# x by wide DMA transposes, the last w1/w3 columns with tokens on partitions, and a new order of the first loads

## The chip, the cores and the metric

The kernel runs on one core of a Trainium2 chip. Each core has five engines that work side by side: TensorE (PE; its weight loads are listed as PEld), VectorE (DVE), ScalarE (ACT), GpSimd (POOL) and SyncE (SP, which here only issues DMAs). Matrix products land in PSUM, from where ScalarE or VectorE must fetch them; DMAs move data between HBM and SBUF. The metric is the device time of one execution in microseconds; the time of a kernel is the median of its runs.

## The reference

Two branches share one input and a learned gate mixes them. All arrays are bf16; S = 2048 tokens, D = 512, F = 1376.

```
x = A_x                                              # [1, 2048, 512]
g = sigmoid((x * gate_w).sum(-1))                    # one number per token
q, k, v = x @ wqkv                                   # 32 heads of 16
a = softmax(mask(q k^T / 4)) v @ wo                  # mask: the last 256 keys, causal
b = (silu(x @ w1) * (x @ w3)) @ w2                   # F = 1376
out = g * a + (1 - g) * b
```

## The kernel before

**Layout.** Everything is computed from xT, x with its 512 features on partitions (four groups of 128, `NDC`) and the 2048 tokens along the free dimension. Tokens are handled in four parts of 512 (`t` or `g`).

- *Projections* (`add_proj`, `add_v`): Q and K come out transposed, 128 features (8 heads, a group `c`) by 512 tokens; V comes out with tokens on partitions. Each is four matmuls of 512 columns, one for each feature group of x. Only in the very first Q and K block, the 512 columns are done as twice 256, so that they can begin with half of the tokens (`spans`).
- *Scores* (`add_burst`): a "burst" is 8 to 12 small matmuls, four row groups of PE at a time, that fill a PSUM tile `big` of four banks. There is only one such tile. ScalarE takes the exponential of 2048 columns at once (L579), POOL or VectorE masks the edges of the window (L170, L589).
- *PV* (`add_pv`): the probabilities times V, 72 or 96 small matmuls; VectorE transposes the result and divides by the sum.
- *MLP* (`add_up`, `add_down`): F is cut into 11 pieces of 128 (`NFC`), the last of 96 (`FL`). For each piece and each 512 tokens, w1 and w3 are the stationary weights, and x's 512 tokens stream past: a tile of F on partitions by tokens, four matmuls each (L447). ScalarE forms tanh(gate/2) (L459), VectorE multiplies twice (L464, L469) and leaves a tile `hT`. The down product then uses 128 tokens of each `hT` as weights and streams w2 past (L502), 11 matmuls for each 128 tokens; piece 10 is last in order in the first part of the tokens, fifth in the others (`FSEQ`).
- *Gate*: `gate_w` is loaded as one more column of w1, so in the last piece 97 columns are used, and row 96 of the tanh tile `ttz` holds the gate's tanh for 512 tokens. It lies along the free dimension, and is needed with tokens on partitions. `add_gate` sends it to DRAM and back through two small DMAs on SP (L410, L414).
- *Output* (`add_out`): the product with wo, then one VectorE instruction that adds the two branches, and a store on SP (L541).

**How x gets transposed.** The first 512 tokens come as two tiles `xs` of 256 tokens in three plain DMAs (`x_dma`, L114); PE transposes them against an identity in 16 matmuls of 128 columns (`add_tx`, L238), and ScalarE and VectorE copy the results to xT (L244, L246). The three other parts come by DMA transpose straight into xT, four instructions of 512 tokens by 128 features each (`xt_dma`, L118).

**What sets the order.** The instruction order of all engines is written out by the kernel's own planner when the program is built. Each piece of work is an `Op` with engines, a planned duration, dependencies, and slots of pools that it takes and releases; `place` simulates the engines and takes the next op by a key. The planner's random moves (`MOVES`, `move`) shift the keys of single ops, and a list of seeds is fixed in the code. The loads have planned landing times (`dma(name, queue, time, ...)`, L133 to L152), which don't bind the chip: on the chip, an engine waits for the semaphore of the DMA. All these first loads are issued by SP in the order in which they stand: x, the first 128 columns of Q's and K's weights (q0, k0), V's weights (v), the rest of Q's and K's (kq), the first 512 columns of w1 and w3 (wa), their rest (wb), then x's part 1 (t1), w2, parts 2 and 3. An SP or ACT queue carries eight semaphores in turn, so that a DMA also waits for the one eight places before it.

While the first loads are under way, PE runs matmuls on constants (`idle_matmuls`, `NWARM` = 10 ahead, `NFILL` = 3 between the first transposes).

Of the kernel before, what the change touches and what calls it, by code (L numbers as in the profile page):

```python
# [19 lines left out]
def kernel(  # L20
# [38 lines left out]
    ident = pp.tile([P, P], BF16, name="ident")  # L59
    w2_sb = pp.tile([P, NFC, D], BF16, name="w2_sb")  # L60
    bsb = pp.tile([P, NT, D], BF16, name="bsb")
    w1_sb = pp.tile([P, NDC, F + 1], BF16, name="w1_sb")
    w3_sb = pp.tile([P, NDC, F], BF16, name="w3_sb")
# [4 lines left out]
    lim = pp.tile([P, 2, 1, HB], BF16, name="lim")  # L68
    scr = pp.tile([P, 2], F32, name="scr")
# [5 lines left out]
    dr = ctx.enter_context(tc.tile_pool(name="dr", bufs=1, space=bass.MemoryType.DRAM))  # L75
    zd = dr.tile([NTC, 512], F32, name="zd")
# [31 lines left out]
    xs_tiles = {}  # L108

    def x_dma(h, m0, m1):  # L110

        if h not in xs_tiles:
            xs_tiles[h] = xp.tile([P, 2, D], BF16, name=f"xs{h}")
        nc.sync.dma_start(out=xs_tiles[h][:, m0:m1, :],  # L114
                      in_=x2d[256 * h + P * m0:256 * h + P * m1, :].rearrange("(m p) d -> p m d", p=P))

    def xt_dma(t, c):
        nc.sync.dma_start_transpose(out=xT[:, c, 512 * t:512 * (t + 1)],  # L118
                                    in_=x2d[512 * t:512 * (t + 1), c * P:(c + 1) * P])

    def w_dma(eng, dst, src, lo, hi, base=0):
        eng.dma_start(out=dst[:, :, lo:hi],  # L122
                      in_=src[:, base + lo:base + hi].rearrange("(c p) f -> p c f", p=P))

# [3 lines left out]
    def dma(name, eng, at, fn):  # L128
# [4 lines left out]
    dma("x0a", "SP", 3.0, lambda: x_dma(0, 0, 1))  # L133
    dma("x0b", "SP", 3.55, lambda: x_dma(0, 1, 2))
    dma("q0", "SP", 4.2, lambda: w_dma(nc.sync, wq_sb, A_wqkv, 0, P))
    dma("x1", "SP", 4.9, lambda: x_dma(1, 0, 2))
    dma("k0", "SP", 5.5, lambda: w_dma(nc.sync, wk_sb, A_wqkv, 0, P, D))
    dma("v", "SP", 7.0, lambda: w_dma(nc.sync, wv_sb, A_wqkv, 0, D, 2 * D))
    dma("kq", "SP", 9.8, lambda: (w_dma(nc.sync, wk_sb, A_wqkv, P, D, D),
                                   w_dma(nc.sync, wq_sb, A_wqkv, P, D)))  # L140
# [3 lines left out]
    dma("wb", "SP", 17.5, lambda: (w_dma(nc.sync, w1_sb, B_w1, FA, F),  # L144
                                   w_dma(nc.sync, w3_sb, B_w3, FA, F)))
    dma("t1", "SP", 20.8, lambda: [xt_dma(1, c) for c in range(NDC)])
    dma("w2", "SP", 24.8, lambda: (
# [3 lines left out]
    dma("t2", "SP", 27.1, lambda: [xt_dma(2, c) for c in range(NDC)])  # L151
    dma("t3", "SP", 29.6, lambda: [xt_dma(3, c) for c in range(NDC)])  # L152
# [21 lines left out]
    def begin():  # L174

        nc.vector.memset(scr[:], 0.0)
        for fn in first_loads:
            fn()
        nc.scalar.activation(out=scr[:, 1:2], in_=scr[:, 0:1], func=ACT.Tanh)
        nc.gpsimd.memset(ident[:], 0.0)  # L180
        nc.gpsimd.affine_select(out=ident[:], in_=ident[:], pattern=[[-1, P]],
                                compare_op=ALU.not_equal, fill=1.0, base=0, channel_multiplier=1)
# [9 lines left out]
        nc.gpsimd.memset(Vaug[:, :, VW - DH:], 1.0)  # L192

# [32 lines left out]
    xT_op = {}  # L226

    def add_tx(m2):

        xT_op[m2] = []  # L230
        for j in range(2):
            key = ("tx", m2, j)
            hold("g", key, 1)

            def pe(key=key, j=j):
                tx = bank(key, BF16, (P, NDC, P))
                for c in range(NDC):
                    nc.tensor.transpose(out=tx[:, c, :], in_=xs_tiles[m2][:, j, c * P:(c + 1) * P],  # L238
                                        identity=ident[:])

            def evac(eng, key=key, j=j):
                dst = xT[:, :, (2 * m2 + j) * P:(2 * m2 + j + 1) * P]
                if eng == "ACT":
                    nc.scalar.copy(out=dst, in_=g_tile[key][:])  # L244
                else:
                    nc.vector.tensor_copy(out=dst, in_=g_tile[key][:])  # L246

            a = Op("PE", 0.22, pe, [loads["x1" if m2 else "x0b" if j else "x0a"]], acq=[("g", key)],
                   kind="tx")
            if (m2, j) == (0, 1):  # L250
                Op("PE", 0.107 * NFILL, lambda: idle_matmuls(NFILL), [a], kind="idle")
            xT_op[m2].append(Op("DVE" if j else "ACT", 0.43 if j else 0.59, evac, [a],
                                rel=[("g", key)], rank=-1))

    def xdep(t0, t1):

        r = []
        for c in range(NDC):
            r.append([xT_op[m // 2][m % 2] if m < 4 else loads[f"t{m // 4}"]
                      for m in range(t0 // P, t1 // P)])  # L260
        return r
# [55 lines left out]
    def add_proj(c, t, is_q):  # L317
# [5 lines left out]

        spans = [(0, 256), (256, 512)] if blk == (0, 0) else [(0, 512)]

        def pe(n0, n1, dc):
            def fn():
                b = bank(key) if (n0, dc) == (0, 0) else g_tile[key]
                nc.tensor.matmul(b[:, n0:n1], lhsT=(wq_sb if is_q else wk_sb)[:, dc, c * P:(c + 1) * P],  # L329
# [39 lines left out]
    def add_v(m):  # L369
# [32 lines left out]
        return a0  # L402

    gate_op = {}
    def add_gate(t, b, tl, row):

        st = {}

# [534 lines left out]
```

## Time and profile before

| What | us |
|---|---|
| Median of 3 runs | 235.07 (234.72 to 235.4) |
| The profiled execution | 234.09 |
| Its span, from the first instruction to the last | 232.4 |
| PE busy | 222.7 (96%) |
| ScalarE busy | 185.5 (80%) |
| VectorE busy | 174.8 (75%) |
| POOL busy | 166.0 (71%) |

The span is cut into 40 slices on the page; a digit is the busy share of an engine in tenths. Groups of instructions are listed as line, engine, operation, output and inputs, shape and count, then busy time in us, the mean of one in ns, and the idle time of the engine before them with what ended it. "issue" is idle time for which the profile shows no cause. A matmul's listed duration runs from its start to its end; matmuls overlap, so that the spacing of their starts is what one costs in a row of them. Rows of the timeline give the start, the time until the last one ends, and how many were merged. Rows "SPq" are DMA issues: the time that SP's sequencer spends on issuing, not the transfer.

### The profile page before, as it was taken

The numbers are of one execution on the slowest core, as the hardware profiler recorded it, in microseconds if no ns is written. First come the engines' busy times: TensorE is split into PE (matmuls) and PEld (weight loads), VectorE is DVE, ScalarE is ACT, GpSimd is POOL, SyncE is SP. The second block draws the span as 40 slices with busy tenths as digits, with TensorE's granted clock in tenths as the row PEclk, the third lists the DMA queues.
The fourth block names the chain that finished last, engine by engine and source line by source line (L and its number), as shares of the span: only waits on it lengthen the run. The fifth ranks groups of instructions, "written<-read, shape, count | busy, mean of one in ns | idle before, by whom it ended". The sixth has DMA issues, their size and how long they took to land.

```text
span 232.4 us, 6996 instructions
## 1 busy us (share of the span) xinstructions
PE 222.7 (96%) x2952; PEld 102.2 (44%) x2985; DVE 174.8 (75%) x296; ACT 185.5 (80%) x169; POOL 166.0 (71%) x323
## 2 busy tenths in 40 slices
PE   7999999999999999999999999999999999999993
PEld 4544443544344443544444444434444444444442
DVE  1497989897999697769969587688978765785622
ACT  3699798998988988987978899897988988893121
POOL 8076688888889887797769777777877879783000
PEclk9999999999999999999999999999999999999999
DMA  5999962000000000000000000000000001000001
GB/s 147 335 367 160 245 131 77 4 1 3 0 25 4 0 13 15 3 24 3 24 3 25 1 3 23 6 23 3 0 27 3 23 4 25 3 25 0 25 34 58
DMA packets 18424, 10.99 MB, mean 47 GB/s; under 512 B 10228, under 2 KB 18388, under 8 KB 18392
## 3 DMA queue, kind: packets, MB, share of 16 engines
q1 hardware_dynamic: 18360, 10.54, 18.4%
q8 instruction: 23, 0.38, 0.7%
q14 instruction: 9, 0.07, 0.1%
q0 software_dynamic: 32, 0.00, 0.1%
HBM read 6.86 MB, written 2.11 MB: 39 GB/s over the span
## 4 chain that ended last, share of the span: by engine, by line
PE 92%; issue 2%; DMA 2%; DVE 1%; SPq 1%; DVEq 0%
PE g L447 34%; PE g L502 16%; PE g L329 12%; PE big L569 11%; PE g L617 8%; PE g L377 6%; PE g L531 5%; DMA wv_sb<-in_A_wqkv_dram 2%; SPq L114 1%; DVE kz L343 1%; SPq L122 0%; DVE ot L538 0%; DVE Vaug L393 0%; DVEq L938 0%; DVEq L538 0%
## 5 line engine op out<-in xcount | busy, mean ns | idle before, releaser
L170 POOL TENSOR_SCALAR_AFFINE_SELECT e<-e 64x256 bf16<-64x256 bf16 (+1 forms) x306 | 160.3, 524 | 44.4 <-ACT e L579 28.2
L579 ACT ACTIVATE e<-big 128x2048 bf16<-128x2048 f32 x76 | 141.0, 1855 | 18.9 <-PE big L569 16.2
L447 PE MATMUL g<-xT,w_sb 128*128 128x512 bf16 (+2 forms) x340 | 84.8, 380 | 2.1 <-issue 1.7
L447 PEld LDWEIGHTS <-w_sb 128*128 128x128 bf16 (+2 forms) x352 | 32.6, 100 | 39.5 <-issue 7.4
L502 PE MATMUL g<-w_sb,hT 128*128 128x512 bf16 (+1 forms) x163 | 40.2, 379 | 1.5 <-issue 1.4
L469 DVE TENSOR_TENSOR hT<-h,g 128x512 bf16<-128x512 bf16 (+1 forms) x44 | 29.8, 680 | 4.4 <-PE g L447 1.6
L628 DVE STREAM_TRANSPOSE t<-g 128x512 f32<-128x512 f32 x32 | 21.4, 698 | 12.8 <-PE g L617 12.8
L464 DVE SCALAR_TENSOR_TENSOR h<-tt,g 128x512 bf16<-128x512 bf16 x40 | 27.0, 682 | 4.1 <-ACT tt L459 3.7
L569 PE MATMUL big<-qp,kz 32*128 32x320 bf16 (+2 forms) x720 | 30.0, 254 | 0.0
L459 ACT ACTIVATE tt<-g 128x512 bf16<-128x512 f32 x40 | 23.5, 596 | 1.8 <-PE g L447 1.5
L502 PEld LDWEIGHTS <-hT 128*128 128x128 bf16 (+1 forms) x176 | 16.1, 97 | 19.7 <-issue 1.1
L569 PEld LDWEIGHTS <-kz 32*128 32x128 bf16 x720 | 10.7, 92 | 31.8 <-issue 31.0
L343 DVE TENSOR_TENSOR kz<-g,maskEO 128x1024 bf16<-128x1024 f32 x16 | 19.5, 1219 | 2.4 <-PE g L329 2.1
L589 DVE TENSOR_TENSOR e<-e,lim 128x256 bf16<-128x256 bf16 x31 | 10.2, 329 | 13.5 <-ACT e L579 13.4
L617 PE MATMUL g<-e,Vaug 64*32 64x320 bf16 (+4 forms) x1440 | 20.3, 253 | 0.0
L508 ACT ACTIVATE bsb<-g,omg 128x512 bf16<-128x512 f32 x13 | 8.9, 686 | 14.1 <-PE g L502 14.0
L393 DVE CAST Vaug<-g 64x256 bf16<-64x256 f32 x40 | 17.1, 427 | 2.9 <-PE g L377 1.9
L617 PEld LDWEIGHTS <-Vaug 64*32 64x32 bf16 x1440 | 16.6, 91 | 3.8 <-issue 1.9
L329 PE MATMUL g<-xT,wq_sb 128*128 128x512 bf16 (+1 forms) x65 | 17.3, 367 | 0.4 <-issue 0.2
L329 PE MATMUL g<-xT,wk_sb 128*128 128x512 bf16 (+1 forms) x65 | 17.2, 367 | 0.3 <-issue 0.2
L538 DVE SCALAR_TENSOR_TENSOR ot<-g,gq,bsb 128x512 bf16<-128x512 f32 (+1 forms) x17 | 11.8, 703 | 7.3 <-PE g L531 5.0
L531 PE MATMUL g<-xs,OT 128*128 128x512 bf16 (+1 forms) x68 | 16.3, 366 | 0.0
(41 smaller groups left out, 117.7 us busy)
## 6 DMA issues: line engine op xcount, KB each, us to landing
out_dram<-ot SPq DMA_DIRECT2D x15, 128.0 KB, 1.7
w_sb<-in_B_w_dram SPq DMA_DIRECT2D x2, 864.0 KB, 10.1
w_sb<-in_B_w_dram SPq DMA_DIRECT2D x1, 1280.0 KB, 6.7
w_sb<-in_B_w_dram SPq DMA_DIRECT2D x2, 512.0 KB, 8.2
wv_sb<-in_A_wqkv_dram SPq DMA_DIRECT2D x1, 512.0 KB
xs<-in_A_wo_dram SPq DMA_DIRECT2D x2, 256.0 KB, 3.0
wk_sb<-in_A_wqkv_dram SPq DMA_DIRECT2D x1, 384.0 KB, 6.1
wq_sb<-in_A_wqkv_dram SPq DMA_DIRECT2D x1, 384.0 KB
```

Source lines behind the costliest of these rows:

```text
L170: nc.gpsimd.affine_select(out=part, in_=part, pattern=[[0, n], [sgn, HB]], compare_op=ALU.is_ge, fill=0.0, base=0 if kind == 0 else -1, ch ...
L329: nc.tensor.matmul(b[:, n0:n1], lhsT=(wq_sb if is_q else wk_sb)[:, dc, c * P:(c + 1) * P], rhs=xT[:, dc, 512 * t + n0:512 * t + n1], start ...
L343: nc.vector.tensor_tensor(out=dst[:], in0=src.to_broadcast(shape), in1=maskEO[:].to_broadcast(shape), op=ALU.mult)
L447: nc.tensor.matmul(b[0:m, :], lhsT=wsb[:, dc, f * P:f * P + m], rhs=xT[:, dc, t * 512:(t + 1) * 512], start=(dc == 0), stop=(dc == NDC - 1))
L459: nc.scalar.activation(out=tl["tt"][0:m, :], in_=g_tile[kg][0:m, :], func=ACT.Tanh, scale=0.5)
L464: nc.vector.scalar_tensor_tensor(out=tl["h1"][0:fs, :], in0=tl["tt"][0:fs, :], scalar=1.0, in1=g_tile[kg][0:fs, :], op0=ALU.add, op1=ALU.mult)
L469: nc.vector.tensor_tensor(out=h_tile[(t, f)][0:fs, :], in0=tl["h1"][0:fs, :], in1=g_tile[ku][0:fs, :], op=ALU.mult)
L502: nc.tensor.matmul(b[:], lhsT=h_tile[(t, f)][0:fs, (m % 4) * P:(m % 4 + 1) * P], rhs=w2_sb[0:fs, f, :], start=(n == 0), stop=(n == NFC - 1))
L531: nc.tensor.matmul(b[:, 0:n], lhsT=OT_tile[m // 4][:, c, (m % 4) * P:(m % 4 + 1) * P], rhs=wo_t[c // 2][:, c % 2, n0:n1], start=(c == 0), ...
L569: nc.tensor.matmul(big[:, u, s0:s0 + step * (w - 1) + 1:step, :], lhsT=k_tile[(c, j // 8)][32 * u:32 * u + 32, j % 8].rearrange("p i x -> ...
L579: nc.scalar.activation(out=e[:, 0:n].rearrange("p s u x -> p u s x"), in_=tl["big"][:, :, 0:n, :], func=ACT.Exp, scale=SCALE)
L617: nc.tensor.matmul(st["o"][r][32 * u:32 * u + 32, o:o + HB * w].rearrange("p (s x) -> p s x", x=HB), lhsT=Vaug[HB * r:HB * (r + 1), j, h0: ...
```

## The change

1. *Transposes.* All four parts of x come by DMA transpose. One instruction now covers several feature groups of 128: `x0` and `x1` are two groups each of the first 512 tokens, and `t1`, `t2`, `t3` are all four groups of a part in one instruction. The PE transposes, the identity, their copies and the 3 filler matmuls are gone; `NWARM` is 13. The first Q and K block is four matmuls of 512 columns each, like the others.
2. *Queues.* SP issues x0 and x1 first. Q's, K's and V's weights are issued by ScalarE, V's in two halves by feature group; each of V's matmuls waits only for its half. In the built program, ScalarE's sixth DMA (the rest of Q's weights) waits for x0's semaphore, and the load of the tanh table and ScalarE's first copies come after it. SP then issues wa, x's part 1 (t1), the rest of w1 (wb1), the rest of w3 (wb3), w2, and parts 2 and 3.
3. *Last piece of w1 and w3.* w1 and w3 lie side by side in one tile `w13`, with a zero column beside w3's last as a partner to the gate's. `add_tail` takes 128 tokens of xT as weights and streams 97 columns of w1 and 97 of w3 past in one matmul of 194 columns; 256 tokens fill one PSUM bank. So the result has tokens on partitions: column 96 is the gate, in the layout in which it is needed, and `add_gate` is gone. The product `hx` is turned back into an `hT` tile by one DMA transpose from SBUF to SBUF on SP. In the first part of the tokens, piece 10 is now eighth in order.
4. *Planner.* Landing times, `COLD`, the planned cost of a mask on VectorE and the seeds in `MOVES` differ, so that the order on every engine is another.

```diff
-    dma("x0a", "SP", 3.0, lambda: x_dma(0, 0, 1))
-    dma("x0b", "SP", 3.55, lambda: x_dma(0, 1, 2))
-    dma("q0", "SP", 4.2, lambda: w_dma(nc.sync, wq_sb, A_wqkv, 0, P))
-    dma("x1", "SP", 4.9, lambda: x_dma(1, 0, 2))
-    dma("k0", "SP", 5.5, lambda: w_dma(nc.sync, wk_sb, A_wqkv, 0, P, D))
-    dma("v", "SP", 7.0, lambda: w_dma(nc.sync, wv_sb, A_wqkv, 0, D, 2 * D))
-    dma("kq", "SP", 9.8, lambda: (w_dma(nc.sync, wk_sb, A_wqkv, P, D, D),
-                                   w_dma(nc.sync, wq_sb, A_wqkv, P, D)))
+    dma("x0", "SP", 3.6, lambda: xt_dma(0, 0, 2))
+    dma("x1", "SP", 5.2, lambda: xt_dma(0, 2, 4))
+    dma("q0", "ACT", 3.6, lambda: w_dma(nc.scalar, wq_sb, A_wqkv, 0, P))
+    dma("k0", "ACT", 4.4, lambda: w_dma(nc.scalar, wk_sb, A_wqkv, 0, P, D))
+    for h in range(2):
+        dma(f"v{h}", "ACT", (6.2, 6.9)[h], lambda h=h: v_dma(h))
+    dma("kq", "ACT", 9.8, lambda: (w_dma(nc.scalar, wk_sb, A_wqkv, P, D, D),
+                                   w_dma(nc.scalar, wq_sb, A_wqkv, P, D)))
...
-    dma("wb", "SP", 17.5, lambda: (w_dma(nc.sync, w1_sb, B_w1, FA, F),
-                                   w_dma(nc.sync, w3_sb, B_w3, FA, F)))
-    dma("t1", "SP", 20.8, lambda: [xt_dma(1, c) for c in range(NDC)])
-    dma("w2", "SP", 24.8, lambda: (
+    dma("t1", "SP", 15.3, lambda: xt_dma(1))
+    dma("wb1", "SP", 18.2, lambda: w_dma(nc.sync, w1_sb, B_w1, FA, F))
+    dma("wb3", "SP", 21.2, lambda: w_dma(nc.sync, w3_sb, B_w3, FA, F))
+    dma("w2", "SP", 25.2, lambda: (
...
-    dma("t2", "SP", 27.1, lambda: [xt_dma(2, c) for c in range(NDC)])
-    dma("t3", "SP", 29.6, lambda: [xt_dma(3, c) for c in range(NDC)])
+    dma("t2", "SP", 27.1, lambda: xt_dma(2))
+    dma("t3", "SP", 29.6, lambda: xt_dma(3))
...
+                nc.tensor.matmul(g_tile[key][:, j], lhsT=xT[:, dc, m * P:(m + 1) * P],
+                                 rhs=w13[:, :, dc, f * P:F + 1], start=(dc == 0),
+                                 stop=(dc == NDC - 1))
...
+                nc.scalar.activation(out=tl["tt"][:, 2 * b:2 * b + 2], in_=g_tile[key][:, :, 0, :],
+                                     func=ACT.Tanh, scale=0.5)
...
+            nc.sync.dma_start_transpose(out=h_tile[(t, f)][:].rearrange("p (j t) -> p j t", j=4),
+                                        in_=hx[:].rearrange("p j f -> p (j f)"))
...
-    FSEQ = [list(range(NFC))] + [[0, 1, 2, 3, NFC - 1] + list(range(4, NFC - 1))] * (NTC - 1)
+    FSEQ = [[*range(7), NFC - 1, *range(7, NFC - 1)]] + [[0, 1, 2, 3, NFC - 1, *range(4, NFC - 1)]] * (NTC - 1)
...
-    NWARM, NFILL = 10, 3
+    NWARM = 13
```

## The prediction

> **What bounds the kernel now.** First the page's first three parts, to see which engine is full and when; then the chain, to see whether the same engine carries the end; then the timeline of the start, where the second part shows the only gap.
>
> ```profile
> PE 222.7 (96%) x2952; PEld 102.2 (44%) x2985; DVE 174.8 (75%) x296; ACT 185.5 (80%) x169; POOL 166.0 (71%) x323
> PE   7999999999999999999999999999999999999993
> DMA  5999962000000000000000000000000001000001
> PE 92%; issue 2%; DMA 2%; DVE 1%; SPq 1%; DVEq 0%
> ```
>
> TensorE (PE) is full in every slice but the first and the last and is 92% of the chain; the others have 47 to 66 us to spare. So there are only two ways to a shorter time: less work for PE, or an earlier start of it. Steady work is regular. Eleven matmuls of 512 columns that follow each other:
>
> ```profile
> 218.00 2.54 PE L502 MATMUL g<-w_sb,hT 128*128 128x512 bf16 x11
> ```
>
> A single one takes 0.38 us from start to end, so ten spacings are 2.54 - 0.38 = 2.16 us: 0.217 us for one, whatever its rows or weight columns. That is the price of the part that goes:
>
> ```profile
> L447 PE MATMUL g<-xT,w_sb 128*97 128x512 bf16 x16 | 4.5, 386 | 0.0
> L447 PE MATMUL g<-xT,w_sb 128*96 128x512 bf16 x16 | 4.5, 384 | 0.0
> ```
>
> These are the last 96 columns of w1 (with the gate's column, 97) and w3. They cost as much as 128 columns.
>
> The start, PE alone:
>
> ```profile
> 0.85 2.29 PE L666 MATMUL big<-const-bfloat16-1.0 128*128 128x256 bf16 x10 [0.85 <-PEq L927]
> 2.99 1.15 PE L238 MATMUL g<-ident,xs 128*128 128x128 bf16 x8
> ...
> 5.57 0.62 PE L238 MATMUL g<-ident,xs 128*128 128x128 bf16 x8 [0.56 <-DMA xs<-in_A_x_dram]
> ...
> 6.79 0.60 PE L329 MATMUL g<-xT,wq_sb 128*128 128x256 bf16 x4
> ...
> 8.08 1.68 PE L377 MATMUL g<-wv_sb,xT 128*128 128x512 bf16 x6 [0.25 <-DMA wv_sb<-in_A_wqkv_dram]
> ...
> 11.21 1.04 PE L329 MATMUL g<-xT,wq_sb 128*128 128x512 bf16 x4
> ```
>
> PE runs from delivery to delivery: x at 2.99 and 5.57, V's weights at 8.08, the rest of the Q and K weights ("kq") at 11.21. From 11.21 on no DMA is named in PE's waits; matmuls and bursts follow each other without a gap to the last one, near 228.6. So all that the start can win or lose is the time of the first kq matmul, and the work done by then.
>
> The queue that feeds the start, and the DMA transposes of later x:
>
> ```profile
> 0.81 0.87 SPq L114 DMA_DIRECT2D xs<-in_A_x_dram  x2
> ...
> 4.91 5.15 SPq L122 DMA_DIRECT2D w_sb<-in_B_w_dram  x4
> 10.11 9.61 SPq L118 DMA_TRANSPOSE xT<-in_A_x_dram  x4
> L118 SPq DMA_TRANSPOSE xT<-in_A_x_dram x12: 1258/1316/3132, 10.1 to 31.5; - x12
> DMA to landing us min/median/max: 2.6/5.2/7.7
> 0.00:5.00 5.00, 4.01 (x22) 2.46 (x22) 0.79 (x4) 2.07 (x3) 4.11 (x13) 1.00 0.59 147
> 5.00:10.00 5.00, 4.14 (x38) 2.55 (x38) 1.65 (x2) 2.00 (x5) 0.77 (x4) 1.00 0.94 295
> ```
>
> One 512x128 transpose holds SP 1.26 us at least and lands 2.6 us (free engines) to 7.7 us (full ones) after its issue. The last two rows are stretches of five microseconds; the number before the GB/s is the share of the DMA engines: 0.59, then 0.94. The first five microseconds are limited by one queue's issues, the next five by the engines.
>
> **The change, part by part.**
>
> *Last columns with tokens on partitions.* Per 512 tokens 8 matmuls of 512 columns become 16 of 194 (97 of w1 and 97 of w3 side by side, xT as weights). Removed: 32 x 0.217 = 6.93 us. Added: 64 of 194 columns. No row has that size; eight of 128 columns at 5.57 are spaced (0.62 - 0.22) / 7 = 0.057 us, four of 256 at 6.79 (0.60 - 0.27) / 3 = 0.109; between them 194 gives 0.084, 5.38 us in all. Bounds: 0.081 (the share of a 512 one) and 0.098 (a weight load's mean, if each were to wait for its own). So PE gains 0.66 to 1.75 us; I take 1.55, since the 128-column row shows loads hidden at 0.057.
>
> What hangs on it: tanh runs on 8 tiles of 194 instead of 4 of 512 columns (2.4 us before; by the slope between 596 ns at 512 and 1878 at 2048, 0.33 each, 2.6). VectorE does 16 steps of 192 columns instead of 8 of 512 (5.4 us): 0.36 each by the slope between 476 ns at 256 and 733 at 512 of the output step, 5.8. Both have idle time enough. The gate no longer goes through DRAM (two DMAs on SP per 512 tokens, whose values nobody on the path waited for). New is one SBUF-to-SBUF DMA transpose per 512 tokens, with down matmuls waiting for it. At 1.3 us issue and 2.6 to 7.7 to landing it is hidden: in the built order 20 us or more of PE work (for the first 512 tokens 14) lie between the last of these matmuls and the first down matmul that reads the tile. On SP only the output stores stand behind it, and PE waits for none of those.
>
> *Warm-up and x's first transposes.* The 16 transposes and 3 fillers on PE go with their evacuations (2 on ScalarE, 2 on VectorE). They lay ahead of 11.21 and are counted there.
>
> *x0 and x1 by DMA transpose, weights on ScalarE's queue.* Two transposes of 512x256 are SP's first issues. Issue of one: between 1.26 us (no dearer than 512x128) and 2.52 (twice the data); I take 1.9, halfway, as one size alone is on record. x1's issue then ends at 0.81 + 3.8 + 0.05 = 4.65; the fastest landing came 2.6 - 1.26 = 1.34 after an issue's end, and twice the data on shared engines adds some 0.5: x1 lands at 6.5. Bounds: 0.81 + 1.3 + 2.6 = 4.7 and 0.81 + 1.3 + 7.7 = 9.8.
> In the built order PE then does 4 matmuls of Q and K on x1, all 16 of V, and the first burst (0.33 us, and 0.1 for the turn into it), before the first kq matmul: 20 x 0.217 + 0.43 = 4.77 us. So by x, kq's first matmul comes at 11.3 (9.5 to 14.6). V's weights in halves let V begin on the first half; with x1 later than 5.2 they are no longer last.
>
> *kq itself.* The same 2 MB are ahead of and in it (x, Q and K, V). Before, kq was in at 11.2 with the large w1/w3 loads behind it in one queue; 1 MB of these ("wa") came 2.9 us later (12.6 and 14.1 in the semaphores' landings). Now they sit in two queues. Gained: up to 0.41 x 5 = 2 us of engine time that one queue's issues left unused. Lost: 0.7, as x moves in 256-byte pieces (18 ns each in the packet records against 50 ns for 1 KB), and up to 2.9 if wa, on SP, gets ahead of kq, on ScalarE. That is 9.9 with none of wa ahead, 12.8 with all. Two queues that share evenly from x1's landing on let most of wa through by the time kq is in; I take 12.0.
> The Trainium skill, DMA: Bandwidth & Descriptors, Rules for kernel authors, speaks against this part: it says that spreading DMAs over SP and ACT doesn't add bandwidth, as they interleave on the same 16 engines, and saves issue time alone. The 0.59 above is such issue time; by that rule alone the sum would take 12.8 for kq.
> ScalarE's last issue waits for x0; its table load (1.28 us) and the copy of Q stand behind that. Even at x0 = 4.8 this ends at 6.8, before Q is ready.
>
> *Sum.* The later one decides: the first kq matmul at 12.0 instead of 11.21, 0.79 us lost. By then PE has done 16 of V's matmuls instead of 12: 4 x 0.217 = 0.87 won. With 1.55 from the tail: 0.87 + 1.55 - 0.79 = 1.63 us.
>
> *x's part 1 ahead of w1's rest, one instruction for four.* By the built order w1's rest is first needed 13.9 us of PE work behind kq, at 26; it landed at 19.9 and now has one 512x512 transpose before it (the four before took SP 9.61 us, held up by the full queue; 5.2 if not). 19.9 + 5.2 = 25.1 at worst: nothing. Part 1 is needed near 42.
>
> *The new order behind it* (the planner's constants and random moves differ). Turns from full matmuls into bursts are 77 in both built orders. Work moves between ScalarE (5 output scalings and 8 of V's copies fewer, 2 Q copies and one K mask more) and VectorE (the reverse, 5 masks fewer), and 10 more mask steps of 0.44 us on POOL: 180, 177 and 170 us by the rows. All stay 40 us under PE. I take 0; a gain is excluded, since PE had no gap to lose; a loss of a few tenths isn't.
>
> The profiled execution took 234.09 us, 1.69 over its span; the median shown is 235.07, 0.98 more. 234.09 - 1.63 = 232.46 for such an execution, 233.4 for a median.
>
> **The rivals.**
> *A: kq isn't held back* (fast). ScalarE issues kq before wa is in the queue, and the idle 41% speaks for it. x and kq allow 9.9; with x1 at 5.2 kq starts at 10.5. Gain 0.87 + 1.55 + 0.7 = 3.1: 232.0.
> *B: wa goes ahead of kq* (no change). 12.8, and some 0.4 more if x's part 1 shares the engines too: kq at 13.2, 0.87 + 1.55 - 2.0 = 0.4 won: 234.7. The full engines from 5 us on speak for it.
> *C: x is starved* (slower). x's 256-byte pieces take turns with ScalarE's 1 KB ones, so that x1 waits for most of that queue. The 7.7 us landing under load is its row; that those transposes were queued behind 1.7 MB speaks against it. The gain is gone when kq starts at 11.21 + 2.42 = 13.63, with x1 at 8.9. At the bound of 9.8 it costs 0.9: 236.0.
> *D: PE stays at half speed* (slower). The ten 256-column warm-ups are spaced 0.21 us, the ones at 6.79 0.109; granted clock reads 1.00 throughout, so the spacing is the evidence. Now 13 warm-ups end at 3.6, and PE idles until x0 at 4.2 or later. If it stays slow for all 20 matmuls behind x1, they cost 4.3 us more, kq starts at 6.5 + 4.77 + 4.3 = 15.6: 237.0. Against it: before, PE also paused, and was fast at 5.57.
> The Trainium skill, TensorE: Matmul & The Clock Gate, What's actually happening, has full clock granted after about 3.4 us of sustained activity, which is D's mechanism.
> *E: the new order stalls* somewhere by 1 us or more: 235.5.
>
> **How the numbers follow.** Likeliest case 0.46, A 0.17, B 0.12, C 0.12, D 0.06, E 0.07. A difference under 0.3% (0.7 us) can hardly be told from none. Faster takes the likeliest and A: 0.63. Same: B and some of E, 0.15. Slower: C, D, the rest of E, 0.22. Forecast 233.4; its own range by PE's 0.66 to 1.75 and kq at 11.3 to 12.8 is 232.6 to 235.1. The range for 8 in 10 goes from 231.7 (a little under A) to 236.2 (C's bound); it leaves out D and the far ends.
>
> **What would show it.** In the profile after: 64 matmuls of 194 columns spaced 0.084; the first kq matmul at 12.0 with a DMA named ahead of it; x1's first matmul at 6.5; SP's first two issues 1.9 us each; the last matmul near 227; no DMA wait of PE behind kq. Wrong if x1 or kq lands behind 13.6, if the Q matmuls on x1 are spaced 0.43, or if PE waits for ScalarE or VectorE in mid-run.

## The result and the profile after

The changed kernel takes 238.03 us (median of four, 237.0 to 238.65) against 235.06 us (234.72 to 235.4): a ratio of 1.0115, with a 95% interval of 1.0081 to 1.015. So it is slower by some 3 us, where 1.6 us faster was forecast, and it lies outside the range. The profiled execution took 237.69 us with a span of 236.0; the one of before had 234.09 and 232.4, so the two traces differ by 3.6 us.

First the page of the changed kernel, the lines that answer to those shown of before, with the row of the granted clock:

```profile
PE 227.0 (96%) x2993; PEld 103.0 (44%) x2993; DVE 176.7 (75%) x307; ACT 180.9 (77%) x162; POOL 169.1 (72%) x333
PE   6599999999999999999999999999999999999994
PEclk9689999999999999999999999999999999999999
DMA  8999950100000000100000000100000010010002
PE 90%; DVE 3%; DMA 3%; issue 2%; SPq 1%; ACT 0%; DVEq 0%; ACTq 0%
```

PE is still what carries the end. Its busy time reads 4.3 us longer, but the two sums can't be compared: before's trace holds 33 matmuls fewer than weight loads (2952 to 2985). So 33 have no record, and they leave 3.4 us of "issue" gaps on PE where the changed kernel's trace has none. What is new in the slices lies in the first three, up to 18 us: PE read 7 and 9 in the first two and reads 6 and 5, and the clock reads 6 and 8 in the second and third, where before it read:

```profile
PEclk9999999999999999999999999999999999999999
```

The timeline of PE's start says more (start, time until the last one ends, what was merged, idle time before and what ended it):

```profile
0.84 2.93 PE L662 MATMUL big<-const-bfloat16-1.0 128*128 128x256 bf16 x13 [0.84 <-PEq L919]
5.28 0.59 PE L290 MATMUL g<-xT,wq_sb 128*128 128x512 bf16 x2 [1.50 <-DMA xT<-in_A_x_dram]
5.71 0.59 PE L290 MATMUL g<-xT,wk_sb 128*128 128x512 bf16 x2
8.96 1.01 PE L290 MATMUL g<-xT,wq_sb 128*128 128x512 bf16 x2 [2.66 <-DMA xT<-in_A_x_dram]
9.77 1.06 PE L290 MATMUL g<-xT,wk_sb 128*128 128x512 bf16 x2
10.62 3.19 PE L338 MATMUL g<-wv_sb,xT 128*128 128x512 bf16 x7
...
14.22 2.12 PE L338 MATMUL g<-wv_sb,xT 128*128 128x512 bf16 x9
16.17 0.38 PE L290 MATMUL g<-xT,wq_sb 128*128 128x512 bf16 x1
```

x1 lets PE go at 8.96, not at 6.5, after 2.66 us of idling. From there on two matmuls take 1.01 us, where the two at 5.28 took 0.59: the spacing is 0.425 us instead of 0.217, until 14.2. The first kq matmul, which the sum hung on, stands at 16.17 instead of 12.0. The windows of the start (PE, PEld, DVE, ACT and POOL busy, granted clock, DMA share, GB/s) show both halves of it:

```profile
0.00:5.00 5.00, 2.93 (x13) 1.93 (x14) 0.37 (x3) 0.00 (x0) 4.13 (x14) 1.00 0.66 142
5.00:10.00 5.00, 2.06 (x7) 0.78 (x7) 0.00 (x0) 1.49 (x2) 0.48 (x3) 0.73 1.14 241
10.00:15.00 5.00, 5.00 (x21) 1.57 (x20) 2.41 (x4) 1.98 (x4) 0.00 (x0) 0.59 1.15 329
```

PE works for 2 of the second five microseconds, on a falling clock. The DMA engines count as full there (1.14), but move 241 GB/s, less than before's 295. In the records full clock is granted from 3.85 to 7.26 us, half from 7.26 to 14.09, and full from then on.

Where the 3.6 us came from can be counted between two matmuls that both kernels have, the first on kq and the first of the twelve that close the work (226.86 before, 230.64 after):

| Term | us |
|---|---|
| First kq matmul, 16.17 instead of 11.21 | +4.96 |
| 16 of V's matmuls ahead of it instead of 12 | -0.87 |
| The tail, 64 x 0.085 instead of 32 x 0.217 | -1.49 |
| The rest: the stretch behind kq is 214.47 us, where 215.65 less these two gains would be 213.29 | +1.18 |
| Start of the closing matmuls | +3.78 |

The forecast's terms were +0.79, -0.87 and -1.55, and nothing behind kq. So of the 5.4 us between forecast and trace, 4.2 were missed in the start (16.17 instead of 12.0), and 1.2 in the order behind it.

### The profile page after: what moved, and what is told of

Same layout as the page of the kernel before. It is cut to its first block, busy times and chain, and to the rows that moved or that the text cites. A ratio compares the mean times of both kernels' runs of the same rounds, so it can differ in the third digit from the quotient of the medians.

```text
span 236.0 us, 7038 instructions
## 1 busy us (share of the span) xinstructions
PE 227.0 (96%) x2993; PEld 103.0 (44%) x2993; DVE 176.7 (75%) x307; ACT 180.9 (77%) x162; POOL 169.1 (72%) x333
## 4 chain that ended last, share of the span: by engine, by line
PE 90%; DVE 3%; DMA 3%; issue 2%; SPq 1%; ACT 0%; DVEq 0%; ACTq 0%
PE g L381 29%; PE g L498 17%; PE g L290 12%; PE big L565 10%; PE g L613 8%; PE g L338 7%; PE g L527 6%; DMA xT<-in_A_x_dram 3%; PE g L431 2%; DVE hT L397 1%; SPq L109 1%; DVE on L633 1%; DVE kz L304 0%; DVE ot L534 0%; DVE OT L638 0%
## 5 line engine op out<-in xcount | busy, mean ns | idle before, releaser
L166 POOL TENSOR_SCALAR_AFFINE_SELECT e<-e 64x256 bf16<-64x256 bf16 (+1 forms) x316 | 163.6, 518 | 46.7 <-ACT e L575 28.3
L381 PE MATMUL g<-xT,w 128*128 128x512 bf16 x320 | 78.7, 380 | 0.4 <-DVE kz L304 0.4
L381 PEld LDWEIGHTS <-w 128*128 128x128 bf16 x320 | 28.9, 98 | 36.3 <-issue 6.7
L498 PE MATMUL g<-w_sb,hT 128*128 128x512 bf16 (+1 forms) x176 | 42.9, 380 | 0.0
L397 DVE TENSOR_TENSOR hT<-h,g 128x512 bf16<-128x512 bf16 x40 | 27.2, 682 | 2.7
L304 DVE TENSOR_TENSOR kz<-g,maskEO 128x1024 bf16<-128x1024 f32 x15 | 18.1, 1207 | 9.5 <-PE g L290 9.4
L354 DVE CAST Vaug<-g 64x256 bf16<-64x256 f32 x48 | 20.3, 423 | 3.9 <-ACT Vaug L352 1.7
L290 PE MATMUL g<-xT,wq_sb 128*128 128x512 bf16 x64 | 17.5, 387 | 4.2 <-DMA xT<-in_A_x_dram 4.2
L290 PE MATMUL g<-xT,wk_sb 128*128 128x512 bf16 x64 | 18.5, 389 | 0.0
L338 PE MATMUL g<-wv_sb,xT 128*128 128x512 bf16 x64 | 18.0, 408 | 0.0
```

The costliest lines, as they stand in the source:

```text
L166: nc.gpsimd.affine_select(out=part, in_=part, pattern=[[0, n], [sgn, HB]], compare_op=ALU.is_ge, fill=0.0, base=0 if kind == 0 else -1, ch ...
L290: nc.tensor.matmul(b[:], lhsT=(wq_sb if is_q else wk_sb)[:, dc, c * P:(c + 1) * P], rhs=xT[:, dc, 512 * t:512 * (t + 1)], start=(dc == 0), ...
L338: nc.tensor.matmul(b[:], lhsT=xT[:, c, m * P:(m + 1) * P], rhs=wv_sb[:, c, :], start=(c == 0), stop=(c == NDC - 1))
L381: nc.tensor.matmul(b[:], lhsT=wsb[:, dc, f * P:(f + 1) * P], rhs=xT[:, dc, t * 512:(t + 1) * 512], start=(dc == 0), stop=(dc == NDC - 1))
L397: nc.vector.tensor_tensor(out=h_tile[(t, f)][:], in0=tl["h1"][:], in1=g_tile[ku][:], op=ALU.mult)
L498: nc.tensor.matmul(b[:], lhsT=h_tile[(t, f)][0:fs, (m % 4) * P:(m % 4 + 1) * P], rhs=w2_sb[0:fs, f, :], start=(n == 0), stop=(n == NFC - 1))
```

## The experiments

For x1's late landing there were three explanations: V's weights, now on ScalarE's queue, take turns with x's pieces on the same engines; the wide transposes are that slow by themselves; or the load of ScalarE's tanh table, which falls into the slump of the DMA rate near 6 us, has to do with it (T in the expectations). For the late kq there are the clock, x1, and kq's own landing (13.79), each of which could set 13.8 to 16.2. Landings below are those of the semaphores. In the first seven kernels the order of the work on each engine is that of the changed kernel; only queues and fillers differ.

**Keeping PE busy.** 22 warm-ups instead of 13, and 25 fillers of 256 columns behind the four matmuls on x0.

```diff
-    NWARM = 13
+    NWARM, NFILL = 22, 25
...
+                if n_proj == 4:
+                    idle_matmuls(NFILL)
```

> The changed kernel with TensorE kept busy through the start: 22 warm-up matmuls instead of 13, and 25 fillers of 256 columns behind the four matmuls on x0, where it idled until x1. No load moves. Theory M (x1 is late because ScalarE's loads share the engines with it, and the idle TensorE then falls to half speed): the matmuls on x1 are spaced 0.217 instead of 0.425, x1 lands at 8.9 as before, and the first kq matmul comes when kq has landed, at 13.8 instead of 16.2; time 238.0 - 2.4 = 235.6. Rival N (the spacing of 0.425 is not from idling but from the DMA traffic or the way x is read): spacing and time stay, 237.5 to 238.5.

236.27 us (235.91 to 237.22), ratio 1.0046 [1.0022, 1.0069]. PE's timeline:

```profile
6.69 2.97 PE L662 MATMUL big<-const-bfloat16-1.0 128*128 128x256 bf16 x25
...
9.92 0.59 PE L290 MATMUL g<-xT,wk_sb 128*128 128x512 bf16 x2
10.36 1.67 PE L338 MATMUL g<-wv_sb,xT 128*128 128x512 bf16 x7
...
14.26 0.39 PE L290 MATMUL g<-xT,wq_sb 128*128 128x512 bf16 x1
```

x1 landed at 8.77, hardly earlier, but its matmuls are spaced 0.217 and the first kq matmul comes 1.91 us earlier, with no load moved (rival N is out). So PE's idling is what brought the clock down. It can't gain more, since kq itself is in at 14.22 only, and the fillers let PE begin on x1 at 9.49: behind the clock stands the next cause, within 0.05 us.

**All first loads in one queue**, SP's, with the order of issue x0, x1, q0, k0, V, kq, wa.

```diff
-        nc.scalar.dma_start(out=wv_sb[:, 2 * h:2 * h + 2, :],
+        nc.sync.dma_start(out=wv_sb[:, 2 * h:2 * h + 2, :],
...
-    dma("q0", "ACT", 3.6, lambda: w_dma(nc.scalar, wq_sb, A_wqkv, 0, P))
+    dma("q0", "ACT", 3.6, lambda: w_dma(nc.sync, wq_sb, A_wqkv, 0, P))
```

> The changed kernel with all first loads on SP, x0 and x1 still first, then q0, k0, V's halves, kq, w1 and w3; ScalarE issues nothing and loads its table at 0.9. Theory M: x1 lands at 5.0 to 5.5 instead of 8.92, kq at 11.5 to 12, no half speed; time 238.0 - 4.4 = 233.6. Rival T (ScalarE's table load, from 5.66 to 6.94 in the changed kernel, holds up the DMA engines and that is what delays x1): the same here, 233.6; the next run tells it from M. Rival S (wide transposes are slow by themselves, the second one waiting for the first): x1 still at 8 to 9, time 236 to 238.

237.19 us, ratio 1.008 [1.0049, 1.011]: a miss, with one half of it right. x1 landed at 5.48 with nothing beside it, against 8.92, so the wide transposes aren't slow by themselves: the sharing is what delays x1. But q0 is now issued at 3.53 and lands at 6.83, and PE stands idle for it and goes on at half speed:

```profile
6.87 1.04 PE L290 MATMUL g<-xT,wq_sb 128*128 128x512 bf16 x2 [3.09 <-DMA wq_sb<-in_A_wqkv_dram]
...
10.26 2.58 PE L338 MATMUL g<-wv_sb,xT 128*128 128x512 bf16 x7
...
15.06 0.38 PE L290 MATMUL g<-xT,wq_sb 128*128 128x512 bf16 x1
```

One cause removed, and another wait with the same consequence put in its place.

**The table load ahead of ScalarE's DMA issues.**

```diff
+        nc.scalar.activation(out=scr[:, 1:2], in_=scr[:, 0:1], func=ACT.Tanh)
...
-        nc.scalar.activation(out=scr[:, 1:2], in_=scr[:, 0:1], func=ACT.Tanh)
```

> The changed kernel with ScalarE's table load ahead of its DMA issues, so that it runs from 0.8 to 2.1; the loads stay on their queues, ScalarE's 1.5 us later. Theory M: ScalarE's loads still share with x1, which lands at 7.5 to 9, kq at 13.5 or later, time 237 to 238.5. Rival T: without the table load among the transfers x1 lands at 5.5 to 6.5, no half speed, kq at 13 to 13.8 (it still shares with w1); time 235 to 235.7.

237.41 us, ratio 1.0085 [1.0055, 1.0116]. x1 lands at 9.27, the half clock lasts from 7.35 to 14.17, the first kq matmul is at 16.39. The table load is out as a cause.

**kq on SP behind x1**, ahead of wa, instead of on ScalarE beside it.

```diff
-    dma("kq", "ACT", 9.8, lambda: (w_dma(nc.scalar, wk_sb, A_wqkv, P, D, D),
-                                   w_dma(nc.scalar, wq_sb, A_wqkv, P, D)))
+    dma("kq", "ACT", 9.8, lambda: (w_dma(nc.sync, wk_sb, A_wqkv, P, D, D),
+                                   w_dma(nc.sync, wq_sb, A_wqkv, P, D)))
```

> The changed kernel with kq alone moved back to SP, behind x1 and ahead of w1 and w3; q0, k0 and V stay on ScalarE, whose table load now comes at about 3.0 to 4.3. Theory M: x1 still shares with V's halves and lands at 7.5 to 8.5, kq no longer shares with w1 and lands at 11 to 12; the matmul on kq comes at 12.5 to 14 by x1, time 234.5 to 236. Rival T: the table load falls on x0, x1 lands at 6 to 7, kq at 11 to 12; time 233.5 to 234.5. If kq's sharing with w1 mattered at all, a run where x1 is early and kq late (above) has to be slower than this one.

237.03 us (236.8 to 238.43), ratio 1.0092 [1.0055, 1.0128]. kq landed at 11.25 instead of 13.79, so wa beside it had cost it 2.5 us. The time doesn't follow: x1 is in at 8.95 and PE is slow until 12.0, so that the first kq matmul stands at 15.22. It also shows that the row of the clock can't be relied on here. On this kernel's page that row reads 9 in every slice but the last, while its matmuls on x0 and x1 are spaced 0.43:

```profile
5.30 1.01 PE L290 MATMUL g<-xT,wq_sb 128*128 128x512 bf16 x2 [1.52 <-DMA xT<-in_A_x_dram]
...
8.99 1.01 PE L290 MATMUL g<-xT,wq_sb 128*128 128x512 bf16 x2 [1.83 <-DMA xT<-in_A_x_dram]
```

**kq on SP and PE kept busy**, the first and the fourth experiment together (both edits as above).

> kq moved back to SP (as in the earlier run that did this alone) and TensorE kept busy with 22 warm-ups and 25 fillers. If late x1, late kq and the half clock are three separate losses: x1 still lands near 8.9, as V's halves still share with it, kq at 11.3, the matmuls on x1 are spaced 0.217, and x1 sets the first kq matmul: 8.9 + 4.8 = 13.7; a gain of 0.5 against the run with fillers alone (14.26), time 235.8 on the base of that call. If kq alone were what holds the start, 11.4 and 233.5.

235.87 us, ratio 1.0028 [1.0012, 1.0044]. kq is in at 11.38, the spacing is 0.217, and the first kq matmul at 14.03 is set by x1 (9.24) alone: 9.28 + 4.77 = 14.05. Of the three causes one is left, and it costs by itself what was left of the loss.

**V and kq on SP, q0 and k0 on ScalarE, 22 warm-ups.** This takes V's and kq's pieces from beside x, keeps q0 early, and needs no fillers, since x1 follows x0 at once.

```diff
-        nc.scalar.dma_start(out=wv_sb[:, 2 * h:2 * h + 2, :],
+        nc.sync.dma_start(out=wv_sb[:, 2 * h:2 * h + 2, :],
...
+    dma("kq", "ACT", 9.8, lambda: (w_dma(nc.sync, wk_sb, A_wqkv, P, D, D),
+                                   w_dma(nc.sync, wq_sb, A_wqkv, P, D)))
...
-    NWARM = 13
+    NWARM = 22
```

> ScalarE issues q0 and k0 alone; V's halves and kq are on SP behind x1 and ahead of w1 and w3. 22 warm-ups, no fillers. Theory M (sharing with ScalarE's loads delays x1): x0 lands at 4.5 to 5, x1 at 5.8 to 6.5, V at 7 to 8, kq at 11.2 to 11.6, no half clock; first kq matmul at 11.3 to 11.7. From before's 11.21 by the sum of the prediction: 0.87 + 1.55 - 0.3 = 2.1 won at the start and in the tail; if the new order of the work behind it costs the 1.0 that the changed kernel's trace shows over its start, 1.1 is left: ratio to before 0.995, 234.0. If the 1.0 was an after-effect of the late start and goes with it: 0.991, 233. Rival S (transposes slow by themselves): x1 at 8 to 9, 236.

This is the fast-start kernel below. 233.62 us (233.48 to 233.76), ratio 0.992 [0.9899, 0.994]: faster than before, and 4.5 us faster than the changed kernel, each taken against the before of its own series. PE's timeline:

```profile
5.61 0.59 PE L290 MATMUL g<-xT,wq_sb 128*128 128x512 bf16 x2 [0.64 <-DMA xT<-in_A_x_dram]
...
6.90 0.59 PE L290 MATMUL g<-xT,wk_sb 128*128 128x512 bf16 x2
7.86 1.76 PE L338 MATMUL g<-wv_sb,xT 128*128 128x512 bf16 x7 [0.36 <-DMA wv_sb<-in_A_wqkv_dram]
...
11.84 0.38 PE L290 MATMUL g<-xT,wq_sb 128*128 128x512 bf16 x1
```

x1 landed at 6.27 and kq at 10.9, at full speed throughout; V's first half, in at 7.82, now sets the pace. The three causes overlap, so that undoing one or two of them gave 1.3 to 2.2 us in the medians (against before in each series), and all three 4.5.

**The same with x0 and x1 as four transposes of 512x128.**

```diff
-    dma("x0", "SP", 3.6, lambda: xt_dma(0, 0, 2))
-    dma("x1", "SP", 5.2, lambda: xt_dma(0, 2, 4))
+    dma("x0", "SP", 3.6, lambda: (xt_dma(0, 0, 1), xt_dma(0, 1, 2)))
+    dma("x1", "SP", 5.2, lambda: (xt_dma(0, 2, 3), xt_dma(0, 3, 4)))
```

> As the run before, but x0 and x1 as two 512x128 transposes each, one feature group in each as in the kernel before. If the issue costs 1.3 us whatever the width (2.65 for two of 512x256 in the changed kernel's trace), four issues end at 6.0 instead of 3.5, V's and kq's issues come 2.6 later, x1 lands at 7 to 8 and kq at 12 to 13: 1 to 1.5 us slower than the run before. If width costs issue time, no difference.

235.82 us, ratio 1.0021 [1.0009, 1.0032], 2.2 us behind the kernel above, where 1 to 1.5 were expected. SP's queue, first of the kernel above, then of this one:

```profile
0.81 2.68 SPq L109 DMA_TRANSPOSE xT<-in_A_x_dram  x2
3.54 1.09 SPq L118 DMA_DIRECT2D wv_sb<-in_A_wqkv_dram  x2
```

```profile
0.81 5.15 SPq L109 DMA_TRANSPOSE xT<-in_A_x_dram  x4
6.00 1.10 SPq L118 DMA_DIRECT2D wv_sb<-in_A_wqkv_dram  x2
```

A transpose costs SP 1.3 us whether it is 128 or 256 columns wide. So V is issued 2.5 us later, PE waits 0.97 us for it behind x1's matmuls, and the first kq matmul comes at 13.44 instead of 11.84. That is 1.6 us in the traces; the other 0.6 of the medians wasn't traced. So of the whole change, the wide form is a clear gain.

**The order behind the start.** The fast-start kernel with the planner's random moves emptied:

```diff
-    MOVES = [80929, 98756, 94876, 67929, 25191, 81224, 35376, 39498, 60517, 91433, 7502, 61184, 42987, 39614, 89372, 28557, 75775]
+    MOVES = []
```

> As the run with V and kq on SP and 22 warm-ups, with the planner's random moves left out, so that the order of the work behind the start is another; to the first up matmul the order is the same, and turns into bursts are 78 instead of 77. If the loss of 1.0 behind the start comes from this one order (theory E), time differs by 0.3 us or more either way, and stalls sit elsewhere. If it comes from the new operations themselves (tail in token layout, wide transposes of parts 1 to 3), it stays: within 0.3 us.

237.42 us, ratio 1.008 [1.0062, 1.0099]. Its first kq matmul is as early as 11.57; the stretch from there to the closing matmuls is 218.56 us, against 214.62 with the moves. An order that isn't fitted costs 4 us here, with the same instructions on PE. This doesn't tell theory E from its rival, since a worse order can stall with any operations.

**An order fitted to the faster start.** The landing times of the fast-start kernel's trace are given to the planner (x0 5.6, x1 6.3, V 7.8 and 8.5, kq 10.9, wa 13.8, and so on), and moves sought anew for them:

```diff
-    dma("x1", "SP", 5.2, lambda: xt_dma(0, 2, 4))
+    dma("x1", "SP", 6.3, lambda: xt_dma(0, 2, 4))
...
-    COLD = 5.5
+    COLD = 4.0
...
+    MOVES = [44140, 12565, 1872, 5768, 75657, 50240, 23319, 55439]
```

> As the run with V and kq on SP and 22 warm-ups (ratio 0.992), with the landing times of that run's trace given to the planner and another set of random moves, so that the order of all work is new; loads, queues and operations are the same. That run still lost 1.96 us behind its first kq matmul (before: 0.48). Theory E (the loss belongs to the order, which was planned for landing times that the chip does not keep): 0.3 to 1.2 us faster, ratio 0.987 to 0.991. Rival (the loss belongs to the new operations, whichever order): 0.991 to 0.994.

233.18 us (233.09 to 233.49), ratio 0.9925 [0.9905, 0.9946]: the same as with the change's own order, within both intervals, and in the rival's range (0.991 to 0.994). So the landing times in the planner weren't what the order lost by.

**The tail alone**, in the kernel before: `w13`, `add_tail` and the new `FSEQ` of the change, with before's loads, PE transposes and queues, before's landing times given to the planner, and moves sought for it.

```diff
+                nc.tensor.matmul(g_tile[key][:, j], lhsT=xT[:, dc, m * P:(m + 1) * P],
+                                 rhs=w13[:, :, dc, f * P:F + 1], start=(dc == 0),
+                                 stop=(dc == NDC - 1))
...
-    MOVES = [14180, 32133, 74601, 10670, 95320]
+    MOVES = [8271, 27519, 12302, 79618, 2925, 70964, 13107, 65452, 66228, 51557, 52990, 65829, 67341, 72188]
```

> The kernel before with one part of the change alone: the last columns of w1 and w3 with tokens on partitions, their DMA transposes, and no trip of the gate through DRAM. x, its PE transposes and all loads stay on SP as before; the planner got before's landing times from the trace and other random moves. The prediction's term: 32 matmuls of 512 columns less, 64 of 194 more, 1.5 us; kq lands at 11.2 as before. Ratio 0.992 to 0.995 if the new order loses no more than before's 0.5 behind kq; 0.997 to 1.0 if the tail brings its own stalls of about 1 us.

235.18 us, ratio 1.0013 [0.9998, 1.0028]: no difference that can be told, and nearest to the second of the two cases expected. Its tail costs the same as in the changed kernel (64 matmuls of 247 ns from start to end), so PE has 1.5 us less to do and doesn't end earlier. The stretch behind kq is 214.56 us; before's 215.65, less 0.87 for V and 1.49 for the tail, less 0.33 for one more burst ahead of kq, would be 212.96. So 1.6 us are lost behind kq, part of it where PE now waits for ScalarE's exponentials:

```profile
165.37 0.40 PE L605 MATMUL big<-qp,kz 32*128 32x256 bf16 x8 [0.48 <-ACT e L615]
171.17 0.40 PE L605 MATMUL big<-qp,kz 32*128 32x320 bf16 x8 [0.33 <-ACT e L615]
```

The start of the kernels with the order of before or of the change side by side, in us (x1 and kq in: landing; first on x1: PE's first matmul on it; stretch: from the first kq matmul to the closing ones; ratios to the kernel before, each measured in one series with it):

| Kernel | x1 in | kq in | first on x1 | spacing there | first on kq | stretch | ratio |
|---|---|---|---|---|---|---|---|
| before | 5.53 | 11.16 | 5.57 | 0.057 (128 columns) | 11.21 | 215.65 | 1 |
| changed | 8.92 | 13.79 | 8.96 | 0.425 | 16.17 | 214.47 | 1.0115 |
| busy PE | 8.77 | 14.22 | 9.49 | 0.217 | 14.26 | 214.61 | 1.0046 |
| one queue | 5.48 | 12.3 | 8.56 | 0.425 | 15.06 | 215.04 | 1.008 |
| table load first | 9.27 | 15.53 | 9.31 | 0.425 | 16.39 | 214.20 | 1.0085 |
| kq on SP | 8.95 | 11.25 | 8.99 | 0.425 | 15.22 | 214.63 | 1.0092 |
| kq on SP, busy PE | 9.24 | 11.38 | 9.28 | 0.217 | 14.03 | 214.63 | 1.0028 |
| V and kq on SP, busy PE | 6.27 | 10.9 | 6.47 | 0.217 | 11.84 | 214.62 | 0.992 |
| the same, narrow transposes | 6.19, 7.65 | 13.18 | 6.91 | 0.217 | 13.44 | 214.65 | 1.0021 |

One thing in this table doesn't add up: the fast-start kernel's span (the last row but one) is 0.6 us under before's in the two traces (231.8 and 232.4), and 1.5 us under it in the medians. Before's own executions of that series lie between 234.41 and 235.99 us, while its profiled one took 234.09; the other's lie between 233.48 and 233.76. What makes before's executions scatter wasn't traced.

## Why the prediction was wrong

The step that failed first is **"x1 lands at 6.5"**. The issue was cheaper than taken, 1.33 us for each of the two instead of 1.9:

```profile
0.81 2.65 SPq L109 DMA_TRANSPOSE xT<-in_A_x_dram  x2
3.52 1.78 SPq L113 DMA_DIRECT2D w<-in_B_w_dram  x2
5.34 8.56 SPq L109 DMA_TRANSPOSE xT<-in_A_x_dram  x1
```

With the engines for itself x1 would have been in at 5.5, as the run with one queue shows. But "twice the data on shared engines adds some 0.5" was wrong by a factor of seven: sharing cost 8.92 - 5.48 = 3.44 us. With kq off ScalarE's queue it lands at 8.95, with V off too at 6.27, so most of this is V's. In the packet records V's 1 KB pieces move from 4.05 us on, and x1's 1024 pieces of 256 bytes from 5.06 (3.57 in the run with one queue) to 8.16. They don't simply take turns: 345 of x1's begin in the first half microsecond, but from 5.5 to 6.5 only 77 of x1's and 43 of V's do, and 16 pieces near 5.5 take over 1 us, where 0.02 and 0.05 are usual. In the four other runs with V beside x1 (busy PE, table load first, kq on SP without and with busy PE) no piece takes that long there, and x1 lands at 8.77 to 9.27 all the same. So that the sharing delays x1 is shown; how the engines choose between the queues isn't.
This is rival C's case, and its break-even of 8.9 was reached; it had been given a chance of 0.12, on the ground that the 7.7 us landing had been measured behind 1.7 MB in one queue.

The second is the **clock, taken at no cost**. Rival D had 0.06, because before, PE had also paused and was fast afterwards. The longest of its pauses in the start was 0.56 us; now there are 1.50 and 2.66, and the second is the wait for x1, C's doing. In the 3.41 us at whose end the clock fell (3.85 to 7.26) PE was busy for 1.02; before, in the 3.41 us that held its pause (4.29 to 7.71), for 2.7. Twenty matmuls and a burst, 4.77 us at full speed, took 16.17 - 8.96 = 7.21: 2.44 us lost, where D had put 4.3, since the clock came back at 14.09 in the midst of them.

The third is **"I take 12.0" for kq**: it landed at 13.79, a microsecond behind the upper bound of 12.8. In the packet records kq's 768-byte pieces and wa's 1024-byte pieces alternate from 10.5 to 13 us at about 95 to 95 in each half microsecond; in the microsecond ahead of that, 335 of wa's begin and 15 of kq's. "Let most of wa through" was rival B's case, and kq on SP gave 11.25, so wa cost 2.5 us, where 2.9 had been put for all of it. B's mechanism was right. Mis-sized was the base under it: "9.9 with none of wa ahead" counts 2 us of engine time that a second queue's issues would win, and with none of wa ahead kq lands at 11.25, or at 10.9 with V on SP too. In the first five microseconds the engines moved 142 GB/s, where before they moved 147.
The Trainium skill, DMA: Bandwidth & Descriptors, Rules for kernel authors, has it that spreading DMAs over SP and ACT doesn't add bandwidth and makes them interleave. The packet records agree, 95 to 95; by that rule alone the prediction had put 12.8, which was nearer than the 12.0 taken.

These three are no sum. The first kq matmul comes at the later of kq's landing (13.79) and of x1's first matmul plus 4.77 us, with what the clock takes on top (8.96 + 4.77 = 13.73, and 16.17 with it). The 4.77 held: 9.28 + 4.77 = 14.05 against 14.03 measured with kq on SP and PE busy, and 6.47 + 4.77 + 0.52 of waiting for V = 11.76 against 11.84 in the fast-start kernel. The break-even of 13.63 was too late, as it took the order behind kq to cost nothing: at 13.44 the kernel with narrow transposes is still slower than before, at 11.84 the fast-start kernel is faster. The chances failed too. C, B and D were counted as rivals that exclude each other, with 0.30 together, while one made the next: ScalarE's V loads delay x1, the wait for x1 takes the clock, and the same sharing holds kq back.

The fourth is **the new order, "I take 0"**. It cost 1.2 us against before's. E was right in its size, and it came beside the other rivals. The place that the changed kernel, the fast-start kernel and the one with the order fitted anew have in common is right behind the first tail; of the changed kernel:

```profile
39.72 1.44 PE L431 MATMUL g<-w,xT 128*128 128x194 bf16 x15
...
42.88 0.81 PE L381 MATMUL g<-xT,w 128*128 128x512 bf16 x3 [0.39 <-DVE kz L304]
```

PE waits for VectorE to give a PSUM bank back. Other stalls of 0.1 to 0.4 us, ended by VectorE as far as the trace names a cause, are at 96, 114, 173 and 174 us; in the kernel with the tail alone ScalarE ends the largest. "All stay 40 us under PE" is true of the sums and says nothing of single moments. Whether the tail's own operations force this, or a better order would be free of it, stays open: each of the three orders with the tail lost 1.1 to 1.6 us, at partly different places, and before's was perhaps merely the best fitted.

What the prediction had right, in the rows of the groups of the changed kernel:

```profile
L431 PE MATMUL g<-w,xT 128*128 128x194 bf16 x64 | 7.0, 247 | 0.0
L439 ACT ACTIVATE ttz<-g 128x194 f32<-128x194 f32 x8 | 2.5, 333 | 0.2 <-PE g L431 0.2
L445 DVE SCALAR_TENSOR_TENSOR h<-ttz,g 128x192 bf16<-128x192 f32 x8 | 2.7, 348 | 1.9 <-ACT ttz L439 1.9
L450 DVE TENSOR_TENSOR hx<-h,g 128x192 bf16<-128x192 bf16 x8 | 2.8, 349 | 0.1
```

The fifteen matmuls at 39.72 are spaced (1.44 - 0.247) / 14 = 0.085 us, where 0.084 was worked out; tanh takes 0.333 (0.33) and the two steps on VectorE 0.35 (0.36). No wait for the tail's SBUF-to-SBUF transposes or for the gate is named on PE, nor for w1's rest behind x's part 1 (19.54 us, needed later): behind kq PE waits for no DMA, as forecast. (Two slips in the working change nothing: 194/512 of 0.217 is 0.082, not 0.081, and with x1 at 5.2 the sum gives 9.97 for rival A's kq, not 10.5.) But a saving on the engine that bounds became time only as far as the order let it: in the run of the tail alone, nothing of it.

## What to carry to other kernels

A load moved to a second queue is no longer behind the urgent one but beside it, on the same engines; here that cost x1 3.4 us and kq 2.5. Put there only what is needed first (here q0 and k0), and keep the rest in the queue behind what PE waits for. Where several deliveries meet in one join, price the latest of them and ask what each lateness brings on (here idling, and with it the clock); undoing one cause in a test then shows only a part of its worth, and that says nothing against it. When work is taken off the busiest engine of a planned order, count the time as won only when a trace shows no new stalls behind it.

## What the runs showed of the hardware

- A DMA transpose cost SP's queue 1.3 us at 512x128 and at 512x256 alike: 5.15 us for four, 2.68 for two.
- In the changed kernel x0's pieces had all moved by 3.9 us, but its semaphore came at 5.24, and x1's pieces only moved from 5.06 on. Alone, in the run with one queue, x1's pieces followed x0's without a gap (3.56 and 3.57), and the two landed at 4.26 and 5.48.
- PE came to full speed at very different times. With 13 warm-ups (2.93 us) it was fast from 3.85 in the changed kernel, but in the run with kq on SP its matmuls were still spaced 0.43 at 5.30, and were until 12.0. With 22 warm-ups it was fast from about 4.0 in the fast-start kernel; in the one with narrow transposes two matmuls at 5.50 still took 1.06 us, though PE had been busy without a break since 0.85 (with the same warm-ups and another order, 1.04 and 0.93).
  The Trainium skill, TensorE: Matmul & The Clock Gate, What's actually happening, says that the gate judges by windows of 3413 ns that run freely and don't start with the kernel. The changed kernel's records agree, 3.41 us of full clock and 6.83 of half; and in all twelve traces each stretch between two recorded changes is a whole number of 3.413 us (1, 2, or 65 to 68). Counted back and forth from the first recorded change, the windows at the start account for every case:

  | Kernel | Window, us | PE busy in it, us | Clock at its end |
  |---|---|---|---|
  | changed | 0.44 to 3.85 | 2.93 | rises to full |
  | changed | 3.85 to 7.26 | 1.02 | falls to half |
  | kq on SP | 1.79 to 5.20 | 1.99 | stays at half |
  | kq on SP, busy PE | 0.07 to 3.48 | 2.63 | rises to full |
  | narrow transposes | -0.22 to 3.19 | 2.35 | stays at half |
  | narrow transposes | 3.19 to 6.61 | 3.41 | rises to full |
  | narrow transposes | 6.61 to 10.02 | 2.04 | stays at full |

  So a window needn't be filled, and the 3.4 us of sustained activity that stand beside rival D weren't needed: 2.63 of 3.41 us raised the clock and 2.35 didn't. It fell after 1.02 and held after 2.04. Where the windows lie differs from trace to trace (the first rise comes between 3.48 and 12.09 us), so that the same warm-up is enough in one and not in another. An estimate from these rows: a warm-up of 5.3 us, split evenly between two windows in the worst case, would have 2.63 us in one of them.
- The row of the granted clock reads full before its first recorded change, even where the spacing of matmuls shows half speed. Of the four executions of the changed kernel two had a mean clock of 0.985 or 0.986 and two (238.65 and 237.0 us) of 1.0, and were no faster for it. At the start of a kernel the spacing is the evidence.
